# Transfers booked by their size in the ordering pass, and products of zeros by constants in TensorE's idle time of the first batch of heads

## The chip, the cores and the metric

One core of a Trainium2 chip runs the whole program in one launch. The metric is the device time in microseconds; the median of three runs of the kernel before is 1121.18 us (1121.18, 1116.87 and 2566.6). The core has five engines with queues of their own, each worked off strictly in order: TensorE (PE: products and transposes into PSUM), VectorE (DVE), ScalarE (ACT), GpSimd (POOL, used only for constants here) and SyncE (SP), which issues all transfers. An instruction that waits for a semaphore holds up everything behind it on its engine.

## The reference

Linear attention over a memory mixed with local causal attention, then two feed-forward layers on all 2304 rows:

```python
B, H, S, D = (4, 8, 576, 64)
scores = np.where(causal, -1e9, scale * q @ k.T)          # per batch and head
a = np.exp(scores - scores.max(-1)); a /= a.sum(-1) + 1e-09
local = a @ v
q_p = np.where(q > 0, q, np.exp(q) - 1.0) + 1.0
mem_out = (q_p @ M_prev) / ((q_p * z_prev).sum(-1) + 1e-06)
x = g * mem_out + (1 - g) * local                          # g = sigmoid(beta), per head
x = x.transpose(0, 2, 1, 3).reshape(B * S, H * D)           # 2304 x 512
h = x @ w_in;  x = (h * np.tanh(softplus(h))) @ w_out       # layer 1: 512 -> 2048 -> 512
h = x @ w_in2; out = (h * np.cos(h)) @ w_out2               # layer 2
```

## The kernel before

**Attention** works on 16 pairs of heads, four pairs for each batch (function `pair`, m = 0 to 15). For a pair, SyncE loads k, q, z, v and M (L328 to L347). PE transposes k and q (`ptk`, `ptq`, L368). In three groups (`slot`, s0, s1, s2) PE forms the scores (`s`, L461; the mask is added by products in bf16, L465; `sx`, L472), VectorE takes their maxima (`nm`, L486), ScalarE the exponentials (`p`, L502), VectorE scales them (L539). PE then transposes the probabilities in blocks of 128 (`t`, L554; 30 blocks in a pair), which ScalarE and VectorE copy to `PT`, and forms the products with the values (`pv`, L621). The result goes by `xs` to DRAM (`x1d`, L630).

**Feed-forward.** The weights of the layers come in an integer form (`raw`, L110 and L113), and VectorE and ScalarE decode each in five operations (`decode_w`, L125 to L142) into two parts; a product by x or by w takes three passes over such parts. The first layer has two halves. `block0` does the first half of its inner dimension for nine blocks of 256 rows: x is loaded from `x1d` (L666), split (ScalarE L285, VectorE L701), multiplied by w_in (`h`, L726), evacuated, put through Mish (ScalarE L738), split again (`G`, L746) and multiplied by w_out (`acc`, L769). A block can start when the pairs of its rows are done: block 0 after pairs 0 to 3. Blocks fill PE while later pairs run through their softmax. `late` does the second half of layer 1 (blocks 9 to 14 of 384 rows; L854, L934) and layer 2 (blocks 15 to 20; L854, L936).

**What sets the order.** Nothing of this is issued as the loops run. Each step is entered by `add` as a task with an engine (or two to choose from), a cost, its predecessors, a rank and the buffers that it takes. `arrange` (L175) then plays the program through: at each time it gives each free engine the ready task of lowest rank, books its cost, and the tasks' functions are called in the order that results. That fixes the order in each engine's queue. A transfer has a cost on SyncE and a `lag` after which its data count as landed, 2.0 to 4.0 us, whatever else is on the way. PE's clock is not part of the plan.

Of the kernel before, what the change touches and what calls it, by code (L numbers as in the profile page):

```python
# [10 lines left out]
F32 = mybir.dt.float32  # L11
F32R = mybir.dt.float32r
I32 = mybir.dt.int32
BF16 = mybir.dt.bfloat16
# [15 lines left out]
def tile_kernel(ctx: ExitStack, tc: tile.TileContext, q, k, v, M_prev, z_prev, beta,  # L30
                moe_w_in, moe_w_out, moe2_w_in, moe2_w_out, out):
    nc = tc.nc
# [3 lines left out]
    P = 128  # L36
# [5 lines left out]
    T0 = 256  # L42
# [54 lines left out]
    pools = {}  # L97
# [57 lines left out]
            made[cls] = self.n + 1  # L155

    class Task:
        __slots__ = ("eng", "cost", "fn", "deps", "rank", "takes", "func", "mode", "lag", "end", "n", "outs", "on")

    tasks = []  # L160
    slots_of = {}

    def add(eng, cost, fn, deps=(), rank=0.0, takes=(), uses=(), func=None, mode=0, lag=0.0):
        t = Task()
        t.eng, t.cost, t.fn, t.rank, t.takes = eng.split("/"), cost, fn, rank, list(takes)
        t.func, t.mode, t.lag, t.end, t.on = func, mode, lag, None, None
        t.deps = [d for d in deps if d is not None]
        for b in (*takes, *uses):
            b.users.append(t)
        tasks.append(t)  # L170
        return t

    SEM, SWITCH, TABLE, WAIT = 0.1, 0.12, 1.3, 2.5

    def arrange():  # L175
        outs = {}
# [20 lines left out]
        func, mode = "exp", 0  # L197
        now, order, left = 0.0, [], len(tasks)


# [13 lines left out]
        while left:  # L214
            nxt = None

            def later(x):
                nonlocal nxt
                if nxt is None or x < nxt:
                    nxt = x  # L220

            for e in ready:
                if free[e] > now:
                    later(free[e])
                    continue
                best = None
                for r in ready[e]:
                    rank, k, at, t = r
                    if t.on is not None:
                        continue  # L230
                    for b in t.takes:
                        f = at_free(b)
                        if f is None:
                            at = None
                            break
                        at = max(at, f)
                    if at is None:
# [12 lines left out]
                t = r[3]  # L250
                cost = t.cost[t.eng.index(e)] if isinstance(t.cost, tuple) else t.cost
                if e == "act" and t.func and t.func != func:
                    cost, func = cost + TABLE, t.func
                if e == "pe":
                    cost, mode = cost + (SWITCH if t.mode != mode else 0.0), t.mode
                t.on, t.end = e, now + cost
                free[e] = t.end
                for b in t.takes:
                    held[b.cls][turn[b.cls] % len(held[b.cls])] = b
                    turn[b.cls] += 1  # L260
                for x in t.eng:
                    ready[x] = [q_ for q_ in ready[x] if q_[3] is not t]
                order.append(t)
                left -= 1
                for d in outs.get(id(t), ()):
                    d.n -= 1
                    if not d.n:
                        put(d)
                later(t.end)
                if e == "host":  # L270
                    later(now)
            if left:
                assert nxt is not None, [(e, r[0], r[3].fn.__name__, [(b.cls, b.n, turn[b.cls]) for b in r[3].takes]) for e in ready for r in ready[e]][:40]
                now = max(now, nxt)
        return order

    def run(order):
        for t in order:
# [35 lines left out]
    x1_done = {}  # L314

    def pair(m):
# [29 lines left out]
            nc.sync.dma_start(out=mv[0:D], in_=M_prev[b, h0:h0 + 2].rearrange("h d e -> d h e"))  # L346
            nc.sync.dma_start(out=mv[D:P], in_=v[b, h0:h0 + 2, 0:D].rearrange("h p d -> p h d"))  # L347

        dk = add("sp", 0.9, f_k, rank=R, takes=[B_["k"]], lag=2.8)
        dq = add("sp", 1.3, f_q, rank=R, takes=[B_["q"]], lag=2.8)  # L350
        dz = add("sp", 0.5, f_z, rank=R + 5, takes=[B_["z"]], lag=2.5)
        dv = add("sp", 1.8, f_v, rank=R + 5, takes=[B_["v"], B_["mv"]], lag=2.5)


        got = {}
# [249 lines left out]
        def pv(x):  # L605
# [30 lines left out]
            x1_done[m, x] = add("sp", 0.4, f_out, [t_x], -1.0, [], [B_["xs"]], lag=2.0)  # L636
            return t_p, t_x

        p_0 = x_0 = None
# [48 lines left out]
    def block0(bi, prev):  # L688
        R = 10000.0 + 1000 * bi
        bx = Buf("x0")  # L690
        ld = add("sp", 0.5, lambda e: load_x(bi), x_ready(bi), -0.5, [bx], lag=3.0)
        sp = []
        for c in (0, 2):
            def f_hi(e, c=c):
# [98 lines left out]
        xa_done[bi] = add("sp", 0.5, lambda e: nc.sync.dma_start(out=xad[bi], in_=d["o"]), [e1], -0.5, [], [bo], lag=2.0)  # L793
        return lasts[1]


# [6 lines left out]
    def late(bi, s0):  # L803
# [24 lines left out]
        if p == 1:  # L828
            def f_xa(e):
                d["o"] = o = O(bi, NKC, T1)  # L830
                t = j * T1
                while t < (j + 1) * T1:
                    b, s_ = divmod(t, T0)
                    w = min(T0 - s_, (j + 1) * T1 - t)
                    nc.sync.dma_start(out=o[:, :, t - j * T1:t - j * T1 + w], in_=xad[b][:, :, s_:s_ + w])
                    t += w

            xa = add("sp", 1.0, f_xa, [t_host2] + [xa_done[b] for b in range(N0)], R0 - 30, [bo], lag=3.5)
        prev = [None] * na
        for k_, f in enumerate(fs):  # L840
            s = s0 + k_
# [100 lines left out]
        for c in range(na):  # L942
# [5 lines left out]
            else:  # L948
# [5 lines left out]
                def f_out(e, c=c):  # L954
# [5 lines left out]
                add("sp", 0.4, f_out, [outs[-1]], -0.5, [], [bo], lag=2.0)  # L960
        if p == 1:
            x2_done[j] = add("sp", 0.4, lambda e: nc.sync.dma_start(out=x2d[j], in_=d["o"]), outs, -0.5, [], [bo], lag=2.0)
# [37 lines left out]
    def f_g1(e):  # L1000
        nc.vector.tensor_scalar(out=ginv, in0=ginv, scalar1=1.0, scalar2=None, op0=ALU.add)

    t_b = add("sp", 0.4, f_beta, rank=0.5, lag=2.0)
    t_g0 = add("act", 0.4, f_g0, [t_b], 0.0, func="exp")
    t_ginv = add("dve", 0.2, f_g1, [t_g0], 0.0)

# [90 lines left out]
```

## Time and profile before

| | |
|---|---|
| runs | 1121.18, 1116.87, 2566.6 us; median 1121.18 |
| profiled execution | 1123.04 us, its span 1121.3 us |
| PE busy | 1068.7 us, 95% of the span |
| DVE, ACT busy | 750.6 us (67%), 578.0 us (52%) |
| DMA | 88.70 MB, mean 79 GB/s |
| chain of waits | PE 80%, DVE 11%, DMA 4%, ACT 3% |

Busy shares are means over the span. Stages are told apart by the pairs and blocks that run in them: pairs 0 to 3 up to 101.2 us, pair 4 and the first products of block 0 to 132.3, pairs 5 to 15 with blocks in between to 388.4, the last blocks of the first half to 515, and then `late`. The clock column of the profile gives PE's granted clock in tenths or hundredths of 2.4 GHz: 1.00 and 0.50 are its two levels, 2.4 and 1.2 GHz.

### The profile page before, as it was taken

To read this page: it belongs to the slowest core of one execution; us is meant where nothing else is said; L and a number is where in the kernel's file an instruction comes from. 1 tells how busy PE (TensorE), PEld (TensorE's weight loads), DVE (VectorE), ACT (ScalarE), POOL (GpSimd) and SP (SyncE) were. 2 spreads that over 40 slices of the span, in tenths; PEclk is the share of its full clock that TensorE was granted. 3 is DMA by queue.
4 is the path that set the end of the run, shared out by engine and by line. 5 is a ranking of instruction groups with operands and counts; after the bars stand their busy time and mean duration, and the time that the engine had idled before them with its cause. 6 is when DMAs were issued, how large, how long until landed. Compare 5 with 4: busy or idle time off the path is not lost.

```text
span 1121.3 us, 17518 instructions
## 1 busy us (share of the span) xinstructions
PE 1068.7 (95%) x6720; PEld 940.4 (84%) x6720; DVE 750.6 (67%) x1684; ACT 578.0 (52%) x1286; POOL 3.8 (0%) x19
## 2 busy tenths in 40 slices
PE   6888989999999989997999999999999999999998
PEld 4555767778787789997999999999999999999997
DVE  6787887787877568416841225898667666666664
ACT  4665666665666434333332333576556455554554
POOL 1000000000000000000000000000000000000000
PEclk9776989999999989999999999999999999999999
DMA  5454322323132156404741123600001010000000
GB/s 142 116 144 125 102 77 50 104 60 100 34 102 54 60 165 201 134 37 149 224 143 52 62 85 122 207 20 29 29 1 57 1 38 20 29 29 1 29 1 29
DMA packets 112852, 88.70 MB, mean 79 GB/s; under 512 B 65792, under 2 KB 103680, under 8 KB 112768
## 3 DMA queue, kind: packets, MB, share of 16 engines
q1 hardware_dynamic: 112768, 87.58, 26.0%
q8 instruction: 53, 0.87, 0.3%
q14 instruction: 31, 0.25, 0.1%
HBM read 68.69 MB, written 18.87 MB: 78 GB/s over the span
## 4 chain that ended last, share of the span: by engine, by line
PE 80%; DVE 11%; DMA 4%; ACT 3%; issue 1%; SPq 1%; ACTq 0%; DVEq 0%
PE h L854 26%; PE acc L936 18%; PE h L726 9%; PE acc L934 7%; PE acc L769 7%; PE t L554 4%; PE pv L621 3%; DVE nm L486 3%; PE s L461 3%; DMA x<-x1d 2%; DVE p L539 1%; PE ptq L368 1%; ACT p L502 1%; DVE PT L287 1%; DMA raw<-in_moe_w_out_dram 1%
## 5 line engine op out<-in xcount | busy, mean ns | idle before, releaser
L854 PE MATMUL h<-x,w 128*128 128x384 f32 x1728 | 345.7, 337 | 1.6 <-ACT g L870 1.6
L854 PEld LDWEIGHTS h<-x,w 128*128 128x128 f32 x1728 | 307.4, 188 | 17.6 <-ACT g L870 1.8
L936 PE MATMUL acc<-w,G 128*128 128x512 f32 x864 | 228.9, 393 | 0.0
L936 PEld LDWEIGHTS acc<-w,G 128*128 128x128 f32 x864 | 159.9, 188 | 21.8
L726 PE MATMUL h<-x,w 128*128 128x256 f32 x864 | 134.3, 296 | 8.3 <-ACT g L285 5.3
L921 DVE TENSOR_TENSOR G<-g,G 128x384 fp32r<-128x384 f32 x144 | 79.8, 555 | 90.8 <-ACT G L285 88.9
L769 PE MATMUL acc<-G,w 128*128 128x256 f32 x864 | 130.5, 291 | 1.7 <-DVE G L746 0.7
L726 PEld LDWEIGHTS h<-x,w 128*128 128x128 f32 x864 | 116.9, 199 | 13.2 <-ACT g L285 8.3
L934 PE MATMUL acc<-G,w 128*128 128x384 f32 x576 | 113.8, 337 | 3.9 <-DVE G L921 2.4
L769 PEld LDWEIGHTS acc<-G,w 128*128 128x128 f32 x864 | 113.1, 193 | 4.9 <-ACT o L285 1.8
L285 ACT ACTIVATE G<-g 128x384 fp32r<-128x384 f32 (+1 forms) x156 | 83.2, 534 | 65.0 <-DVE g L905 34.6
L502 ACT ACTIVATE p<-s,nm 128x64 f32<-128x64 f32 (+4 forms) x160 | 81.3, 516 | 47.7 <-DVE nm L486 20.1
L934 PEld LDWEIGHTS acc<-G,w 128*128 128x128 f32 x576 | 100.8, 188 | 5.4 <-DVE G L921 3.5
L554 PE MATMUL t<-ident,p 128*128 128x128 f32 (+1 forms) x480 | 86.3, 314 | 15.4 <-ACT PT L285 5.2
L554 PEld LDWEIGHTS t<-ident,p 128*128 128x128 f32 (+1 forms) x480 | 61.4, 160 | 29.4 <-ACT PT L285 11.8
L882 DVE TENSOR_SCALAR u<-hs 128x384 f32<-128x384 f32 x96 | 34.5, 359 | 71.3 <-ACT hs L285 68.6
L898 ACT ACTIVATE n<-n 128x384 f32<-128x384 f32 x96 | 50.2, 523 | 60.7 <-DVE n L894 60.7
L461 PE MATMUL s<-kT,qT 64*128 64x448 f32 (+4 forms) x320 | 68.7, 513 | 12.2 <-DVE nm L486 6.5
L486 DVE TENSOR_REDUCE nm<-s 128x2 f32<-128x1024 f32 (+4 forms) x80 | 62.5, 791 | 19.8 <-PE s L465 10.2
L905 DVE TENSOR_TENSOR g<-n,hs 128x384 f32<-128x384 f32 x96 | 53.3, 555 | 28.5 <-ACT n L901 28.4
L285 ACT ACTIVATE PT<-t 128x512 f32<-128x512 f32 (+3 forms) x100 | 46.9, 480 | 41.3 <-PE t L554 40.1
L870 ACT ACTIVATE g<-h 128x384 f32<-128x384 f32 x48 | 23.3, 488 | 84.7 <-PE h L854 83.9
(88 smaller groups left out, 1183.9 us busy)
## 6 DMA issues: line engine op xcount, KB each, us to landing
raw<-in_moe_w_in_dram SPq DMA_DIRECT2D x32, 512.0 KB, 4.4
raw<-in_moe_w_out_dram SPq DMA_DIRECT2D x32, 512.0 KB, 4.4
k<-in_k_dram SPq DMA_DIRECT2D x32, 144.0 KB, 2.8
x1d<-xs SPq DMA_DIRECT2D x32, 144.0 KB, 2.0
xad<-o SPq DMA_DIRECT2D x9, 512.0 KB, 2.8
x2d<-o SPq DMA_DIRECT2D x6, 768.0 KB, 3.2
x<-x2d SPq DMA_DIRECT2D x6, 768.0 KB, 4.3
out_dram<-o SPq DMA_DIRECT2D x18, 256.0 KB, 2.0
```

The costliest lines, as they stand in the source:

```text
L285: nc.scalar.activation(dst, src, AF.Copy, scale=1.0 if scale is None else scale)
L461: nc.tensor.matmul(o[:, j], qT[pr, s0:s0 + P], kT[pr, 0:main], start=True, stop=False)
L486: nc.vector.tensor_reduce(out=s["nm"][:, c], in_=s["sp"][i], axis=AX.X, op=ALU.max, negate=True)
L502: nc.scalar.activation(d["p", i][:, j, D + lo:D + hi], src, AF.Exp, bias=s["nm"][:, c, j:j + 1], scale=1.0, accum_out=s["sm"][:, 1 if part ...
L554: nc.tensor.transpose(ps[:, at:at + r], d["p", i][0:r, h, j * P:(j + 1) * P], ident[0:r, 0:r])
L726: nc.tensor.matmul(h[:, half // 2], w[:, a, 0, c * P:(c + 1) * P], x[:, e_, c, :], start=c == 0 and pi == 0, stop=c == NKC - 1 and pi == 2)
L769: nc.tensor.matmul(t[:, c], w[:, a, 1, n * P:(n + 1) * P], G[:, e_, half], start=f == 0 and pi == 0 and c == 0, stop=f == NFH - 1 and pi == 2,
L854: nc.tensor.matmul(q_["h"], w[:, a, 0, c * P:(c + 1) * P], x[:, e_, c, :], start=c == 0 and pi == 0, stop=c == NKC - 1 and pi == 2)
L905: nc.vector.tensor_tensor(out=q_["g"], in0=q_["n"], in1=q_["hs"], op=ALU.mult)
L921: ENG[e].tensor_tensor(out=q_["G"][:, 1], in0=q_["g"], in1=q_["G"][:, 0].bitcast(F32), op=ALU.subtract)
L934: nc.tensor.matmul(o, w[:, a, 1, c * P:(c + 1) * P], G[:, e_, :], start=st, stop=sp_)
L936: nc.tensor.matmul(o, G[:, a, c * P:(c + 1) * P], w[:, e_, 1, :], start=st, stop=sp_)
```

## The change

Two things are changed in the ordering pass. First, a transfer has a `size` in KB in place of a fixed lag: transfers are booked one after the other at 160 KB per us, and each counts as landed 2.0 us after its turn. Second, as long as no block of the feed-forward has begun, the pass looks at what it has given PE in the time just before; where this falls under a share, and no task is ready, it puts in a product of a constant by zeros, with 256 columns in bf16, into a PSUM buffer that nothing reads. The computation of the outputs is the same. All engines get another order, since the booked times differ.

```diff
+    RATE, LAND = 160.0, 2.0
...
                 if best is None:
+                    if e == "pe" and t_warm.on and not turn["h"]:
+                        while done and done[0][1] < now - 3.4:
+                            done.popleft()
+                        if sum(y - max(x, now - 3.4) for x, y in done) < 0.75 * 3.4:
+                            t = Task()
+                            t.eng, t.cost, t.fn, t.on, t.end = ["pe"], 0.12, f_dummy, "pe", now + 0.12
+                            free[e] = t.end
+                            done.append((now, t.end))
+                            order.append(t)
+                            later(t.end)
                     continue
...
+                if e == "pe":
+                    done.append((now, t.end))
+                if t.size:
+                    moved = max(moved, t.end) + t.size / RATE
+                    t.lag = moved - t.end + LAND
...
+    def f_warm(e):
+        warm["w"] = pools["h"].tile([P, 2, T0], F32, tag="h", name="warm")
+        warm["z"] = const.tile([P, T0], BF16, name="zeros")
+        nc.vector.memset(warm["z"], 0.0)
+
+    def f_dummy(e):
+        nc.tensor.matmul(warm["w"][:, 0], ident_b, warm["z"], start=True, stop=True)
+
+    t_warm = add("dve", 0.2, f_warm)
...
-        dk = add("sp", 0.9, f_k, rank=R, takes=[B_["k"]], lag=2.8)
-        dq = add("sp", 1.3, f_q, rank=R, takes=[B_["q"]], lag=2.8)
+        dk = add("sp", 0.9, f_k, rank=R, takes=[B_["k"]], size=288)
+        dq = add("sp", 1.3, f_q, rank=R, takes=[B_["q"]], size=352)
...
-        ld = add("sp", 0.5, lambda e: load_x(bi), [*need, t_host if bi == N0 else t_host2], R0 - 90, [bx], lag=3.5)
+        ld = add("sp", 0.5, lambda e: load_x(bi), [*need, t_host if bi == N0 else t_host2], R0 - 90, [bx], size=768)
...
-        ld = add("sp", 0.5, lambda e: fetch_next(), after, rank - 30.0, [bw], lag=4.0)
+        ld = add("sp", 0.5, lambda e: fetch_next(), after, rank - 30.0, [bw], size=512)
```

The other transfers are changed in the same way (z 64, v 320, `x1d` 144, x of block0 512, `xad` 512, `o` from `xad` 768, `x2d` 768, output rows 256 KB).

There are 187 products of zeros: 22 ahead of the transposes of the first keys, 12 ahead of those of the first queries, 120 in the rest of pairs 0 to 3, in runs of up to 19, and 33 in pair 4, up to the first product of block 0. Numbers in the names below are pair or block and part.

SyncE, the transfers after the first loads of pair 1, before (`raw0_1_1` is a part of the weights, `xs0` the result of pair 0):

```order
L328 DMA k2_337<-in_k_dram 96x6x64 x2
L338 DMA z2_381<-in_z_prev_dram 128x128
L332 DMA q2_421<-in_q_dram 128x2x64
L334 DMA q2_421<-in_q_dram 128x4x64 x2
L113 DMA raw0_1_1_437<-in_moe_w_out_dram 128x1024
L630 DMA x1d0_65<-xs0_446 128x288
```

and with the change:

```order
L358 DMA k2_400<-in_k_dram 96x6x64 x2
L113 DMA raw0_1_1_448<-in_moe_w_out_dram 128x1024
L362 DMA q2_511<-in_q_dram 128x2x64
L364 DMA q2_511<-in_q_dram 128x4x64 x2
L660 DMA x1d0_65<-xs0_508 128x288
L368 DMA z2_536<-in_z_prev_dram 128x128
```

The weights stand ahead of the queries of pair 2 now, and z of pair 2 behind the first result of pair 0.

PE, pair 4 from its last scores before (`h0_0` are block 0's first units, `t4` the transposes of pair 4's probabilities):

```order
L461 MATMUL s4_2_1197<-kT4_976,qT4_1098 128x192 x2
...
L726 MATMUL h0_0_0_1222<-x0_1169,w0_0_435 128x256 x12
L726 MATMUL h0_0_0_1222<-x0_1169,w0_1_642 128x256 x12
L554 MATMUL t4_3_1264<-ident_85,p4_0_1173 128x128 x4
L368 MATMUL ptk5_1_1272<-ident_85,k5_1013 128x96 x3
L726 MATMUL h0_0_1_1282<-x0_1169,w0_2_874 128x256 x6
L554 MATMUL t4_3_1294<-ident_85,p4_0_1173 128x128 x4
L726 MATMUL h0_0_1_1282<-x0_1169,w0_2_874 128x256 x6
L726 MATMUL h0_0_1_1282<-x0_1169,w0_3_925 128x256 x12
L554 MATMUL t4_0_1329<-ident_85,p4_0_1173 128x64 x2
L554 MATMUL t4_4_1332<-ident_85,p4_1_1176 128x128 x4
```

and with the change (`warm` are the products of zeros; of each run the first stands):

```order
L491 MATMUL s4_2_1374<-kT4_1112,qT4_1255 128x192 x2
...
L303 MATMUL warm_171<-zeros_172,ident_b_120 128x256
...
L584 MATMUL t4_3_1411<-ident_85,p4_0_1333 128x128 x4
...
L584 MATMUL t4_3_1440<-ident_85,p4_0_1333 128x128 x4
L584 MATMUL t4_0_1446<-ident_85,p4_0_1333 128x64 x2
...
L584 MATMUL t4_4_1478<-ident_85,p4_1_1336 128x128 x2
L756 MATMUL h0_0_0_1482<-x0_1325,w0_0_452 128x256 x6
```

Before, 24 products of block 0 stood ahead of the first transposes of `p4` and 84 ahead of the end of `pv4`; now none and 24. At the end of `pv15`, the last of the attention, 840 products of the first half stood ahead before, and now 834, of 1728.

ScalarE, after the last result of the attention, before (x9 is the x of the first late block, x6 that of block 6, `g0_5_0<-h0_5_0` the evacuation of PE's first unit of block 5):

```order
L285 ACTIVATE xs15_4596<-pv15_1_4603 128x288
L285 ACTIVATE g0_4_2_4614<-h0_4_3_4627 128x512
L738 ACTIVATE g0_4_2_4614<-g0_4_2_4614 128x1024
L285 ACTIVATE x9_4668<-x9_4668 128x768 x2
L285 ACTIVATE x6_4697<-x6_4697 128x512
L285 ACTIVATE g0_5_0_4745<-h0_5_0_4703 128x512
```

and with the change:

```order
L315 ACTIVATE xs15_4780<-pv15_1_4783 128x288
L315 ACTIVATE g0_4_2_4815<-h0_4_2_4744 128x512
L315 ACTIVATE g0_4_2_4815<-h0_4_3_4835 128x512
L768 ACTIVATE g0_4_2_4815<-g0_4_2_4815 128x1024
L315 ACTIVATE G0_4_2_4906<-g0_4_2_4815 128x512
L140 ACTIVATE w0_8_4916<-dec0_8_0_4888 128x512
L315 ACTIVATE g0_5_0_4934<-h0_5_0_4890 128x512
L140 ACTIVATE w0_8_4916<-dec0_8_1_4944 128x512
L315 ACTIVATE o4_4992<-acc0_4_0_4808 128x512
L140 ACTIVATE w0_9_4996<-dec0_9_0_4960 128x512
L768 ACTIVATE g0_5_0_4934<-g0_5_0_4934 128x1024
L315 ACTIVATE x9_4852<-x9_4852 128x768 x2
```

The evacuation of `h0_5_0` stood behind the casts of x9 and x6; now they stand behind it, with weight casts (`w0_8`, `w0_9`) between. In the same way the cast of x10 stood ahead of the activations g3 and g4 and stands behind them now, and the subtractions for x0 and x1 on VectorE moved from among the scaling of pair 4's first scores to behind it.

## Rows read from the trace of the kernel before

**Rows 1.** Stages: length; busy PE, PEld, DVE, ACT, POOL (count); clock; DMA share; GB/s.

```profile
0.00:31.60 31.60, 22.69 (x107) 13.95 (x107) 21.71 (x61) 15.71 (x45) 3.84 (x19) 1.00 0.51 128
31.60:50.20 18.60, 14.43 (x97) 9.32 (x95) 14.83 (x42) 11.60 (x36) 0.00 (x0) 0.76 0.46 124
50.20:77.20 27.00, 24.84 (x154) 15.40 (x153) 23.27 (x58) 16.64 (x49) 0.00 (x0) 0.73 0.43 116
77.20:101.20 24.00, 20.59 (x120) 12.80 (x116) 18.75 (x48) 13.64 (x40) 0.00 (x0) 0.64 0.43 118
101.20:132.30 31.10, 27.34 (x200) 22.17 (x198) 25.68 (x64) 18.42 (x45) 0.00 (x0) 0.84 0.47 129
132.30:388.40 256.10, 241.38 (x2003) 192.44 (x2000) 200.87 (x527) 161.46 (x439) 0.00 (x0) 0.99 0.28 73
388.40:411.00 22.60, 17.94 (x120) 17.54 (x121) 11.07 (x20) 7.55 (x12) 0.00 (x0) 0.85 0.59 187
...
501.00:565.00 64.00, 56.75 (x345) 54.46 (x344) 45.77 (x85) 26.11 (x46) 0.00 (x0) 1.00 0.58 184
565.00:1121.30 556.30, 552.75 (x2885) 514.74 (x2884) 339.38 (x700) 275.32 (x525) 0.00 (x0) 1.00 0.14 48
```

**Rows 2.** The same view, the stretches where matmuls run at the lower clock.

```profile
4.40:30.90 26.50, 21.99 (x97) 13.49 (x99) 20.42 (x55) 14.43 (x44) 0.22 (x2) 1.00 0.51 131
41.60:54.40 12.80, 11.20 (x49) 7.39 (x49) 11.17 (x30) 7.44 (x23) 0.00 (x0) 0.50 0.25 63
65.00:74.80 9.80, 9.42 (x41) 5.88 (x41) 8.32 (x22) 5.47 (x14) 0.00 (x0) 0.50 0.35 93
82.10:98.80 16.70, 14.84 (x68) 9.51 (x68) 14.27 (x41) 10.20 (x32) 0.00 (x0) 0.50 0.25 78
...
401.50:410.00 8.50, 6.47 (x31) 6.47 (x32) 6.53 (x11) 3.74 (x7) 0.00 (x0) 0.60 0.21 66
```

**Rows 3.** Timeline of PE: start, duration, instruction; in brackets the idle time before.

```profile
4.41 1.19 PE L368 MATMUL ptk<-ident,k 96*128 96x96 f32 x6 [4.41 <-DMA k<-in_k_dram]
...
7.74 1.86 PE L461 MATMUL s<-kT,qT 64*128 64x448 f32 x4 [0.47 <-ACT qT L285]
...
31.59 1.02 PE L461 MATMUL s<-kT,qT 64*128 64x448 f32 x4
...
65.21 2.92 PE L554 MATMUL t<-ident,p 64*128 64x64 f32 x12 [0.80 <-DVE PT L287]
...
71.94 1.23 PE L621 MATMUL pv<-PT,mv 128*64 128x288 f32 x4
...
403.53 1.65 PE L726 MATMUL h<-x,w 128*128 128x256 f32 x6 [3.97 <-ACT g L285]
...
530.78 2.18 PE L934 MATMUL acc<-G,w 128*128 128x384 f32 x11 [2.37 <-DVE G L921]
```

**Rows 4.** The chain of waits in order of time: start, duration, what.

```profile
32.31 5.27 DMA raw<-in_moe_w_out_dram
...
394.98 7.30 DMA x<-x1d
...
405.17 1.28 PE acc L769 x6
...
411.17 0.71 PE acc L769 x6
```

**Rows 5.** Timeline of DVE (columns as in rows 3).

```profile
1.33 0.55 DVE L77 CAST ident_b<-ident 128x128 bf16<-128x128 f32 x1 [0.47 <-POOL ident masks.py:199]
...
37.68 0.43 DVE L125 TENSOR_SCALAR dec<-raw 128x512 int32<-128x512 int32 x1 [0.88 <-DMA raw<-in_moe_w_out_dram]
...
110.69 1.29 DVE L701 TENSOR_TENSOR x<-x 128x512 fp32r<-128x512 f32 x2 [1.97 <-ACT x L285]
...
526.29 1.83 DVE L822 TENSOR_TENSOR x<-x 128x768 fp32r<-128x768 f32 x2 [5.51 <-ACT x L285]
```

**Rows 6.** Timeline of ACT (columns as in rows 3).

```profile
399.12 1.58 ACT L285 ACTIVATE x<-x 128x768 fp32r<-128x768 f32 x2 [3.09 <-DMA x<-x1d]
```

More of the change, by code (lines that the diff above doesn't have):

```diff
@@ L157, in tile_kernel, with add @@
     class Task:
-        __slots__ = ("eng", "cost", "fn", "deps", "rank", "takes", "func", "mode", "lag", "end", "n", "outs", "on")
+        __slots__ = ("eng", "cost", "fn", "deps", "rank", "takes", "func", "mode", "lag", "end", "n", "size", "on")
     tasks = []
     slots_of = {}
-    def add(eng, cost, fn, deps=(), rank=0.0, takes=(), uses=(), func=None, mode=0, lag=0.0):
+    def add(eng, cost, fn, deps=(), rank=0.0, takes=(), uses=(), func=None, mode=0, lag=0.0, size=0):
         t = Task()
         t.eng, t.cost, t.fn, t.rank, t.takes = eng.split("/"), cost, fn, rank, list(takes)
-        t.func, t.mode, t.lag, t.end, t.on = func, mode, lag, None, None
+        t.func, t.mode, t.lag, t.end, t.on, t.size = func, mode, lag, None, None, size
         t.deps = [d for d in deps if d is not None]
@@ L196, in arrange @@
         free = {e: 0.0 for e in ready}
-        func, mode = "exp", 0
+        func, mode, moved = "exp", 0, 0.0
+        done = deque()
         now, order, left = 0.0, [], len(tasks)
@@ L275, in arrange @@
         return order
+    warm = {}
+    def f_warm(e):
[5 more added lines that the diff above has]
+    t_warm = add("dve", 0.2, f_warm)
     def run(order):
@@ L347, in f_v @@
             nc.sync.dma_start(out=mv[D:P], in_=v[b, h0:h0 + 2, 0:D].rearrange("h p d -> p h d"))
-        dk = add("sp", 0.9, f_k, rank=R, takes=[B_["k"]], lag=2.8)
-        dq = add("sp", 1.3, f_q, rank=R, takes=[B_["q"]], lag=2.8)
-        dz = add("sp", 0.5, f_z, rank=R + 5, takes=[B_["z"]], lag=2.5)
-        dv = add("sp", 1.8, f_v, rank=R + 5, takes=[B_["v"], B_["mv"]], lag=2.5)
+        dk = add("sp", 0.9, f_k, rank=R, takes=[B_["k"]], size=288)
+        dq = add("sp", 1.3, f_q, rank=R, takes=[B_["q"]], size=352)
+        dz = add("sp", 0.5, f_z, rank=R + 5, takes=[B_["z"]], size=64)
+        dv = add("sp", 1.8, f_v, rank=R + 5, takes=[B_["v"], B_["mv"]], size=320)
         got = {}
@@ L635, in pv @@
             t_x = add("act/dve", c_both(w), f_xs, [t_p, x_0], R + 60, [B_["xs"]] if x == 0 else [], [bm] + ([B_["xs"]] if x else []))
-            x1_done[m, x] = add("sp", 0.4, f_out, [t_x], -1.0, [], [B_["xs"]], lag=2.0)
+            x1_done[m, x] = add("sp", 0.4, f_out, [t_x], -1.0, [], [B_["xs"]], size=144)
             return t_p, t_x
@@ L690, in block0 @@
         bx = Buf("x0")
-        ld = add("sp", 0.5, lambda e: load_x(bi), x_ready(bi), -0.5, [bx], lag=3.0)
+        ld = add("sp", 0.5, lambda e: load_x(bi), x_ready(bi), -0.5, [bx], size=512)
         sp = []
@@ L792, in block0 @@
         e1 = add("act/dve", c_both(512), lambda e: f_o(e, 1), [lasts[1], e0], RM + bi, [], [ba[1], bo])
-        xa_done[bi] = add("sp", 0.5, lambda e: nc.sync.dma_start(out=xad[bi], in_=d["o"]), [e1], -0.5, [], [bo], lag=2.0)
+        xa_done[bi] = add("sp", 0.5, lambda e: nc.sync.dma_start(out=xad[bi], in_=d["o"]), [e1], -0.5, [], [bo], size=512)
         return lasts[1]
@@ L836, in f_xa @@
                     t += w
-            xa = add("sp", 1.0, f_xa, [t_host2] + [xa_done[b] for b in range(N0)], R0 - 30, [bo], lag=3.5)
+            xa = add("sp", 1.0, f_xa, [t_host2] + [xa_done[b] for b in range(N0)], R0 - 30, [bo], size=768)
         prev = [None] * na
@@ L959, in late @@
                                 [ba[c]] + ([bo] if c else [])))
-                add("sp", 0.4, f_out, [outs[-1]], -0.5, [], [bo], lag=2.0)
+                add("sp", 0.4, f_out, [outs[-1]], -0.5, [], [bo], size=256)
         if p == 1:
-            x2_done[j] = add("sp", 0.4, lambda e: nc.sync.dma_start(out=x2d[j], in_=d["o"]), outs, -0.5, [], [bo], lag=2.0)
+            x2_done[j] = add("sp", 0.4, lambda e: nc.sync.dma_start(out=x2d[j], in_=d["o"]), outs, -0.5, [], [bo], size=768)
     slots_of.update({"q": 1, "k": 1, "v": 2, "z": 1, "mv": 2, "mn": 1, "ph": 2, "den": 3, "qT": 2, "kT": 2, "kd": 2, "PT": 1,
@@ L1001, in f_g1 @@
         nc.vector.tensor_scalar(out=ginv, in0=ginv, scalar1=1.0, scalar2=None, op0=ALU.add)
-    t_b = add("sp", 0.4, f_beta, rank=0.5, lag=2.0)
+    t_b = add("sp", 0.4, f_beta, rank=0.5, size=4)
     t_g0 = add("act", 0.4, f_g0, [t_b], 0.0, func="exp")
```

## The prediction

> **What bounds the kernel now.** I read the stages first [rows 1], because the share of busy time over the whole span (PE 95%) mixes stages with different limits. From 565 us to the end TensorE is busy 552.75 of 556.30 us: no order can shorten that half. The loss lies before 132 us, around the end of the attention (388 to 411: 17.94 of 22.60 busy) and where the first feed-forward pass ends (501 to 565: 56.75 of 64.00). In the 101.2 us of pairs 0 to 3 PE is busy 82.55 us, and a good part of that at half speed: in the stretches of [rows 2] it is busy 21.99, 11.20, 9.42 and 14.84 us while the clock is at 0.50, which is the 1.2 GHz level. In the first of them the clock column says 1.00, but the durations don't: four products of queries and keys took 1.86 us at 7.74 and 1.02 us at 31.59 [rows 3]. So some 57 us of PE's work ran at the lower level; at the higher it would be about 29 us shorter. VectorE is the next limit there: busy 21.71, 14.83, 23.27 and 18.75 us, so it leaves 22.6 us idle in 101.2 [rows 1]. No change of PE alone can take more than that from pairs 0 to 3.
>
> The second loss is that engines stand behind a transfer that the planner thought would be there sooner. The chain of waits has such pieces: a weight transfer from 32.31 to 37.6 and an x transfer from 394.98 to 402.3 [rows 4]. VectorE waits for the first until 37.68, 0.88 us with nothing to do, and a reduction of scores stands behind it in its queue. At 110.69 it waits 1.97 us for x [rows 5]. At 399.12 ScalarE waits 3.09 us for x9 [rows 6], with the evacuation that PE needs queued behind, so that PE waits 3.97 us and then works at the lower level until 410 [rows 2, 3]: six products took 1.28 us at 405.17 and 0.71 at 411.17 [rows 4].
>
> **The change, part by part.** It does two things in the ordering pass, and nothing to the computation: 187 products of zeros on PE, and another order on all engines. Prices against the profiled run, 1123.04 us for a span of 1121.3; that is 1.9 over the median of the runs, 1121.18.
>
> A product of zeros has 256 columns and a weight load of its own, like the products in [rows 4]: 0.71/6 = 0.12 us at the higher clock, 1.28/6 = 0.21 us at the lower.
>
> (a) The start. The identity is cast by 1.88 us [rows 5], so PE can begin zeros at about 2.1 us. 22 of them at 0.21 end at 6.8 us, where the keys were transposed from 4.41 us on [rows 3]; 12 more stand ahead of the queries: 1.4 to 2.6 us. The first scores come 3.8 to 5 us later. If the clock is up by then they win back 0.84 us on each of the two large groups (1.86 against 1.02) and a little on the small ones, 2 us in all. Between +3 and 0 (VectorE's first idle hides it); I take +1.5, near the middle, since the scores start the chain of the whole pair.
>
> (b) The weight transfer of pair 1 is now issued ahead of the next queries, not behind them. VectorE's wait goes. It is worth 0 to -3.8, all the idle time of VectorE in the stage 31.6 to 50.2 [rows 1]; I take the middle, -2, since the transfer's 5.27 us [rows 4] began only behind the queries. Queued behind it on SyncE are now the next queries, which pair 2 needs a pair later.
>
> (c) The clock in pairs 0 to 3. From above -22.6 (VectorE's idle), from below 0. The zeros stand mainly ahead of a pair's third group of scores and ahead of its first transposes; among the last twenty transposes of a pair, where the lower clock lasted, there are only 4 to 6 of them. So I expect the clock to hold through the scores and the first transposes and to fall later: half of the 29 us of PE's time. VectorE was busy 77 to 87% of the same stretches [rows 2], so less than half of it shortens the path: -6.
>
> (d) 120 zeros stand within pairs 0 to 3 beside those of the start: 14.4 us at the higher level, 25.6 at the lower. PE's idle time from 4.41 to 101.2 us is 14.2 us [rows 1]; that is their cover. They run as soon as PE reaches them, not when it would idle, so a run of ten can outlast its wait: +1.5, between 0 and +11.4 (25.6 - 14.2).
>
> (e) Pair 4 and the first block of the feed-forward. Before, 84 of its products lie ahead of the end of pair 4; now 24, and zeros stand where they were. The stage 101.2 to 132.3 then becomes like pair 3's, 24.0 us, less some 2.5 us from clock, plus 24 x 0.12 = 2.9 for the products: 24.4 against 31.1, -6.7. That also contains the wait for x at 110.69, whose subtraction is now behind the work on pair 4's scores. But the 60 products are owed: at the end of the attention 834 are done against 840, so pairs 5 to 15 take in 54 more, 6.5 us. That stage has 14.7 us of PE idle [rows 1], and some of them fall into it: +4.5 (0 to +6.5). Together -2.2, between +6.5 (pair 4 as long as before) and -6.7 (the idle time takes the 54).
>
> (f) The end of the attention. ScalarE now evacuates the first unit of block 5 before the casts of x9 and x6. PE's wait of 3.97 us goes, and with it the lower clock after it: 6.47 us of PE work from 401.5 to 410 [rows 2], half of it 3.2. What is late next is the decode of the first weights after the attention, which keeps VectorE at work until about the time the next unit needs it. -6 of 7.2; between -7.2 and 0.
>
> (g) The end of the first pass. ScalarE's cast of x10 moves behind two activations, so that VectorE's 5.51 us of idle before x10 [rows 5] no longer holds back the operand for which PE waited 2.37 us [rows 3]. Weight decodes take the cast's place on ScalarE, and they have transfers of their own: -2, between -3.8 and +2.
>
> (h) The rest of the order from 565 us on: nothing, PE being the bound with 3.6 us of idle in 556.
>
> Sum: +1.5 - 2 - 6 + 1.5 - 2.2 - 6 - 2 = -15.2 us. The profiled run would take 1107.8 us, the median about **1106 us**, 1.4% less. About 2% is what a measurement of this kernel can tell from no change: below 1098.8 or above 1143.6.
>
> **The clock and the transposes.** The planner counts every instruction of PE as activity, transposes too. Rows speak against it: from 65.0 to 74.8 us PE was busy 9.42 of 9.80 us at 0.50, with transposes from 65.21 on, and the clock stayed down until after the products of probabilities and values had begun at 71.94 [rows 2, 3]. With products alone, from 403.53 us on, it was up by 411.17 [rows 3, 4]. The Trainium skill says the same ("TensorE: Matmul & The Clock Gate", Part 4: PE-mode transpose): a transpose does not count as a busy PE in the way a product does. By that rule the zeros, sparse where the transposes are, could not hold the clock there; by the planner's own count they hold it throughout. By that rule the sum is rival 2's, by the planner's count rival 1's; my (c) stands between the two.
>
> **Rivals.**
> 1. The zeros hold the clock through pairs 0 to 3, and VectorE becomes the bound. For it: at the higher clock the zeros are 14.4 us, as much as PE's idle time. Against it: the stretch from 65.0 us. Then (c) is some 15 of the 22.6 us and (d) nothing: -25.7, about 1096 us. 0.15.
> 2. The clock falls in each pair as early as before, as transposes don't hold it. Then (c) is 0 or nearly, the rest as above: -9.2, about 1112 us. For it: the stretches of 65.0 and 82.1 us [rows 2]; against it: six to ten zeros now stand ahead of the third group of scores of three of these pairs, where none of them is near a transpose of probabilities. 0.17. It is what the Trainium skill's rule would make of it.
> 3. The transfers' new places only move the waiting: at 394 and 516 us the decode of the weights, for which VectorE is busy 45.77 of 64 us at 501 to 565, ends last instead of x. (f) and (g) are nothing: -7.2, about 1114 us. 0.12. That the order does not do what it says would look the same.
> 4. Slower than before: the clock stays at the lower level and the zeros are in the way. The 153 zeros after the first 34 are 32 us at 0.21, and their cover is 14.2 us of idle time in pairs 0 to 3 and 3.8 in pair 4 [rows 1]; they decide from where a run ends after the operand it fills for, some 2 us for ten. With +14.6 in (d), +3 in (a), 0 in (c), +4.5 in (e), -2 in (b) and -4 in (f) and (g): +16.1, about 1137 us. For it: many of the runs stand between transposes; against it: zeros are products, and a run of products did bring the clock up. 0.06.
>
> **Chances.** My forecast has 0.50. The range reaches from rival 1 to just above the old time, with the bounds of (d) and (e) against (c): 1092 to 1123 us. Faster by over 2%: most of rival 1 and a rest of the forecast's lower end, 0.15. Slower by over 2%: half of rival 4, 0.03. Within 2%: 0.82.
>
> **What would show it.** (a): keys transposed at 6 to 7 us, first exponential after 12.31. (b): no wait for raw weights before 40 us. (c): the clock at full level in the scores of pairs 1 to 4 and at 0.50 in the last transposes and first value products; the end of pair 3 at about 96 us instead of 101.2. (d): runs of zeros that end before their successor's operand. (e): the first feed-forward product only after 105 us, pair 4 done near 120. (f): no gap of PE over 1 us and no 0.50 between 380 and 410 us. (g): no wait of 2 us behind x10. It is wrong if the end of pair 3 does not move, or if PE's gap at the end of the attention only changes its releaser.

## The result, and the profile after

The changed kernel takes **1092.42 us** (median of four runs, 1091.78 to 1094.71); the kernel before took 1120.86 on the same chip. The ratio is **0.9762, 95% interval [0.9731, 0.9792]**: 2.4% faster, where 1.4% was forecast. Medians here and below take in a single far slower run where one fell (before 2566.6 us, first experiment 1175.19, third 1698.83), while the ratios leave it out. The profiled run takes 1091.78 us for a span of 1090.0, 31.3 us less than the span of before; some 2 us of that are the profiled run of before, which lay above its median.

Four lines of the page after: span, busy time, TensorE's clock in the 40 slices, the shares of the chain of waits.

```profile
span 1090.0 us, 17872 instructions
...
PE 1056.5 (97%) x6907; PEld 937.7 (86%) x6907; DVE 761.1 (70%) x1699; ACT 570.6 (52%) x1272; POOL 3.9 (0%) x19
...
PEclk9999999999999999999999999999999999999999
...
PE 85%; DVE 10%; ACT 3%; issue 1%; POOL 0%; ACTq 0%; POOLq 0%
```

A 9 in the clock's line means 0.9 or more; the one stretch at 0.50 behind the start lies at 44.7 to 48.1 us, in pair 1. No transfer is left in the chain (4% before). The stages after, in the columns of [rows 1]:

```profile
0.00:32.90 32.90, 26.47 (x204) 18.76 (x204) 23.48 (x64) 15.44 (x47) 3.87 (x19) 1.00 0.55 141
32.90:48.90 16.00, 13.42 (x105) 9.78 (x103) 14.84 (x41) 10.89 (x35) 0.00 (x0) 0.89 0.54 141
48.90:72.40 23.50, 20.98 (x175) 13.67 (x175) 22.67 (x59) 14.69 (x45) 0.00 (x0) 1.00 0.40 107
72.40:93.10 20.70, 17.24 (x145) 11.49 (x143) 19.38 (x49) 13.63 (x42) 0.00 (x0) 1.00 0.52 143
93.10:119.40 26.30, 23.28 (x201) 16.40 (x198) 25.55 (x64) 16.93 (x53) 0.00 (x0) 1.00 0.66 162
119.40:369.10 249.70, 241.77 (x2031) 195.37 (x2029) 199.98 (x525) 163.73 (x431) 0.00 (x0) 1.00 0.28 73
369.10:391.00 21.90, 21.21 (x169) 20.45 (x170) 12.52 (x22) 9.74 (x15) 0.00 (x0) 1.00 0.65 211
...
539.00:1090.00 551.00, 547.48 (x2856) 509.56 (x2854) 350.33 (x720) 271.68 (x516) 0.00 (x0) 1.00 0.15 50
```

Three stages of [rows 1] had a clock of 0.64 to 0.76; now one of the first four is at 0.89 and the others at 1.00. The waits of the engines for transfers up to 540 us come down to one line, a decode of VectorE at 374 us, around which PE is nowhere idle for more than 0.69 us (engine, line, what it waited for: us in total, times, longest):

```profile
DVE dec L125 <- DMA raw<-in_moe_w_in_dram: 5.7, 1, 5.7
```

Before, up to 565 us, ScalarE waited 22.4 us for x in ten places, and VectorE 9.4 for weights and 5.8 for queries.

The table gives each stage against the forecast, and the third experiment, which has exactly the order of after without the zeros. So "order" is its difference to before, "zeros" what is left. Pairs end here with their last product by the values, up to 0.2 us off the marks of [rows 1]:

| stage | before | after | change | order | zeros | forecast |
|---|---|---|---|---|---|---|
| pairs 0 to 3 | 101.2 | 93.2 | -8.0 | -2.2 | -5.8 | (a) to (d): -5 |
| pair 4 | 31.1 | 26.2 | -4.9 | -2.7 | -2.2 | (e): -6.7 |
| pairs 5 to 15 | 256.1 | 249.7 | -6.4 | -4.9 | -1.5 | (e): **+4.5** |
| to the store of the last block of the first half | 127.3 | 120.7 | -6.6 | -6.5 | -0.1 | (f): -6 |
| to the end | 605.6 | 600.2 | -5.4 | -5.4 | 0 | (g): -2 |
| span | 1121.3 | 1090.0 | -31.3 | -21.7 | -9.6 | -15.2 |

Each column is one execution, and the first row of "order" is not firm: the tenth experiment has the order of before up to there, and its pair 3 ended at 95.2 us, not at 101.2 (see the last section).

### The profile page after: what moved, and what is told of

Same layout as the page of the kernel before. It is cut to its first block, busy times and chain, and to the rows that moved or that the text cites. A ratio compares the mean times of both kernels' runs of the same rounds, so it can differ in the third digit from the quotient of the medians.

```text
span 1090.0 us, 17872 instructions
## 1 busy us (share of the span) xinstructions
PE 1056.5 (97%) x6907; PEld 937.7 (86%) x6907; DVE 761.1 (70%) x1699; ACT 570.6 (52%) x1272; POOL 3.9 (0%) x19
## 2 busy tenths in 40 slices
DMA packets 112852, 88.71 MB, mean 81 GB/s; under 512 B 65792, under 2 KB 103680, under 8 KB 112768
## 3 DMA queue, kind: packets, MB, share of 16 engines
q1 hardware_dynamic: 112768, 87.58, 26.9%
## 4 chain that ended last, share of the span: by engine, by line
PE 85%; DVE 10%; ACT 3%; issue 1%; POOL 0%; ACTq 0%; POOLq 0%
PE h L884 28%; PE acc L966 18%; PE acc L964 9%; PE h L756 9%; PE acc L799 8%; PE pv L651 4%; PE t L584 4%; DVE nm L516 3%; PE s L491 3%; DVE p L569 2%; ACT p L532 1%; PE ptq L398 1%; DVE PT L317 1%; PE warm L303 1%; DVE p L545 1%
## 5 line engine op out<-in xcount | busy, mean ns | idle before, releaser
L884 PEld LDWEIGHTS h<-x,w 128*128 128x128 f32 x1728 | 307.3, 188 | 17.2 <-ACT g L900 1.8
L756 PE MATMUL h<-x,w 128*128 128x256 f32 x864 | 128.9, 288 | 2.7 <-ACT g L315 1.6
L756 PEld LDWEIGHTS h<-x,w 128*128 128x128 f32 x864 | 111.6, 190 | 6.9 <-ACT g L315 4.5
L532 ACT ACTIVATE p<-s,nm 128x448 f32<-128x448 f32 (+4 forms) x160 | 81.4, 517 | 43.7 <-DVE nm L516 16.4
L584 PE MATMUL t<-ident,p 128*128 128x128 f32 (+1 forms) x480 | 74.1, 280 | 10.5 <-DVE PT L317 6.3
L516 DVE TENSOR_REDUCE nm<-s 128x2 f32<-128x128 f32 (+4 forms) x80 | 62.4, 793 | 21.8 <-PE s L495 11.2
L935 DVE TENSOR_TENSOR g<-n,hs 128x384 f32<-128x384 f32 x96 | 53.2, 555 | 26.3 <-ACT n L931 26.2
L584 PEld LDWEIGHTS t<-ident,p 128*128 128x128 f32 (+1 forms) x480 | 53.3, 142 | 21.2 <-DVE PT L317 8.8
L491 PE MATMUL s<-kT,qT 64*128 64x512 f32 (+4 forms) x320 | 61.8, 472 | 9.6 <-DVE nm L516 5.9
L315 ACT ACTIVATE hs<-h 128x384 f32<-128x384 f32 x96 | 47.1, 490 | 39.2 <-PE h L884 36.5
```

The lines of the kernel that those rows point to most:

```text
L315: nc.scalar.activation(dst, src, AF.Copy, scale=1.0 if scale is None else scale)
L491: nc.tensor.matmul(o[:, j], qT[pr, s0:s0 + P], kT[pr, 0:main], start=True, stop=False)
L516: nc.vector.tensor_reduce(out=s["nm"][:, c], in_=s["sp"][i], axis=AX.X, op=ALU.max, negate=True)
L532: nc.scalar.activation(d["p", i][:, j, D + lo:D + hi], src, AF.Exp, bias=s["nm"][:, c, j:j + 1], scale=1.0, accum_out=s["sm"][:, 1 if part ...
L584: nc.tensor.transpose(ps[:, at:at + r], d["p", i][0:r, h, j * P:(j + 1) * P], ident[0:r, 0:r])
L756: nc.tensor.matmul(h[:, half // 2], w[:, a, 0, c * P:(c + 1) * P], x[:, e_, c, :], start=c == 0 and pi == 0, stop=c == NKC - 1 and pi == 2)
```

## The experiments

All run beside the kernel before; ratios are to it, with 95% intervals. Spans and stages are of each one's profiled run. Line numbers are those of the kernel after, or shifted by one to four (those of the kernel before in the tenth).

**1 to 3: the two parts, and the zeros in a fixed order.**

```diff
 e1_sizes_only, against after
-                    if e == "pe" and t_warm.on and not turn["h"]:
+                    if False:
 e2_zeros_only, against after (each of 13 transfers)
-        dk = add("sp", 0.9, f_k, rank=R, takes=[B_["k"]], size=288)
+        dk = add("sp", 0.9, f_k, rank=R, takes=[B_["k"]], lag=2.8)
 e3_order_no_zeros, against after
     def f_dummy(e):
+        return
```

> The transfers are booked by size as in the changed kernel, and no zeros are inserted (the planner chooses its own order without them: 12 feed-forward products ahead of the end of pair 4). Theory A (the zeros' clock gives what pairs 0 to 4 won, the booking what came after): pair 3 ends at 99 to 102 us, the stage of pair 4 is 26 to 28 us long, pairs 5 to 15 about 250 us, the first half of the program ends 11 to 15 us after the changed kernel's; 1103 to 1107 us. Theory B (the booking gives nearly all, the clock was never on the path because VectorE is): pair 3 ends at 94 to 96 us; 1092 to 1096 us. Theory C (the zeros give nearly all, the booking only moves waits): 1115 to 1121 us.

> The zeros are inserted as in the changed kernel, the transfers have the fixed delays of the kernel before again. Theory A: pair 3 ends at 93 to 95 us with the clock at its higher level in nearly all of it, VectorE again waits for the weight transfer near 32 us, pairs 5 to 15 take 253 to 256 us as before, and the gap at the end of the attention is back; 1105 to 1110 us. Theory B: pair 3 ends at 99 to 101 us although the clock is up; 1117 to 1121 us. Theory C: 1092 to 1097 us.

> Exactly the changed kernel's order on every engine, but the 187 products of zeros are not issued. That takes the clock away and nothing else. Theory A: in pairs 0 to 3 the clock is at 0.50 in the transposes again, pair 3 ends at 99 to 101 us instead of 93.1, pair 4's stage is 1 to 3 us longer than 26.3, and from 119 us on nothing differs; 1100 to 1104 us. Theory B: pair 3 ends at 93 to 95 us; 1091 to 1094 us. That the zeros were in the way on balance would show as a time under 1090.

Measured: booking alone 1109.36 us, 0.9912 [0.9875, 0.9949]; zeros alone 1112.76, 0.9939 [0.9908, 0.9969]; the order of after without its zeros 1101.61, 0.9836 [0.9776, 0.9897]. Theory A holds for the third (pair 3 ends at 99.0) and fails for the first two: each part alone gives 0.6 to 0.9%, both 2.4%. In a fixed order the zeros are worth 8 to 9 us (9.2 by the medians, 1101.61 - 1092.42, which come from two series of runs; 8.3 by the two ratios); the rest is order. The first and the third both run without zeros, and differ by 8 us by order alone: pairs 0 to 3 end at 103.6 us instead of 99.0, and without zeros in the plan 918 feed-forward products fall into pairs 5 to 15 instead of 810, and the stage takes 273.1 us instead of 251.2. At 0.15 us a product (129 us for 864) the 108 more are 16 us, so some 6 us are lost there, with a fall of the clock near 215 us; the other stages make up for part of it. Why that order fits worse stays open.

What the zeros do in the fixed order is seen in pair 0. Windows (columns of [rows 1]) of the third experiment, then of the kernel after:

```profile
24.00:27.00 3.00, 2.74 (x12) 1.73 (x10) 2.83 (x8) 1.43 (x4) 0.00 (x0) 0.50 0.57 175
27.00:30.00 3.00, 3.00 (x12) 1.52 (x13) 2.23 (x5) 1.55 (x4) 0.00 (x0) 0.50 0.04 8
```

```profile
24.00:27.00 3.00, 2.65 (x18) 1.75 (x18) 2.98 (x9) 1.77 (x4) 0.00 (x0) 1.00 0.32 96
27.00:30.00 3.00, 2.84 (x25) 1.92 (x24) 3.00 (x7) 1.98 (x5) 0.00 (x0) 1.00 0.21 82
```

PE's timeline after, there:

```profile
22.60 1.36 PE L303 MATMUL warm<-zeros,ident_b 128*128 128x256 bf16 x11
23.89 1.36 PE L584 MATMUL t<-ident,p 64*128 64x64 f32 x10
25.50 1.50 PE L584 MATMUL t<-ident,p 128*128 128x128 f32 x8 [0.25 <-ACT PT L315]
27.17 0.44 PE L584 MATMUL t<-ident,p 128*128 128x128 f32 x2 [0.16 <-ACT PT L315]
27.44 0.38 PE L303 MATMUL warm<-zeros,ident_b 128*128 128x256 bf16 x2
27.66 0.38 PE L584 MATMUL t<-ident,p 128*128 128x128 f32 x2
```

Eleven zeros (0.12 us each) stand ahead of the pair's last 22 transposes and only two within them, and the clock holds through all of them. Without the zeros PE is as busy at 0.50, and gets 12 instructions done in each 3 us instead of 18 and 25.

**4 and 5: the price of zeros.**

```diff
 e4_no_zeros_at_start: f_dummy returns for its first 34 calls
 e8_zeros_doubled: f_dummy issues its product twice
```

> The changed kernel's order, without the first 34 products of zeros (22 ahead of the keys' transposes, 12 ahead of the queries'). If the start's zeros cost what my term (a) said, the keys are transposed at about 4.4 us again instead of 6.69, the first scores come 1 to 2.5 us sooner though at the lower clock (1.86 us instead of 1.02 for four), and pair 0 ends 1 to 2 us sooner: 1090 to 1091.5 us. If they pay for themselves by the clock, pair 0 ends at the same time or later: 1092 to 1094 us.

> The changed kernel's order with every product of zeros issued twice: 187 more, 22 us of TensorE's time at 0.12 us each. If zeros lie in time that TensorE has to spare beside VectorE (my term d near its lower bound), pair 3 ends at 93 to 96 us and the time is 1092 to 1096 us. If they are in the way (the mechanism of my rival 4), about half or more of the 22 us appears: pair 3 ends after 100 us and the time is 1102 to 1114 us.

Measured: 1091.54 us, 0.975 [0.9711, 0.9789], and 1099.78, 0.9851 [0.9814, 0.9887]. Without the first 34 the first exponential starts at 12.01 us, with them at 13.12, yet pair 0 ends at 33.4 and 33.0: the start's zeros win back by the clock what they cost, and no more. Doubled zeros cost 7.9 us of the span, and neither range of their expectation holds: pair 3 ends at 99.7. Of the 7.9 us 5.3 are there by the end of pair 0 (2.8 by its first scores, which start at 12.93 instead of 10.18). From there to the end of pair 4 the doubled kernel, then the one after:

```profile
38.30:127.30 89.00, 84.34 (x727) 61.05 (x727) 82.75 (x210) 55.95 (x174) 0.00 (x0) 1.00 0.50 135
```

```profile
33.00:119.40 86.40, 74.83 (x617) 51.23 (x617) 82.34 (x210) 56.13 (x174) 0.00 (x0) 0.98 0.53 139
```

110 more products make PE busy 9.5 us longer and the stretch only 2.6: behind pair 0 the zeros lie for the most part in time that PE has to spare.

**6 to 9: which transfers, and whether size matters.**

```diff
 e5_x_booked_only (e6_x_not_booked: with "not"); the fixed lags stand beside the sizes
                     moved = max(moved, t.end) + t.size / RATE
+                    if t.takes and t.takes[0].cls in ("x0", "x", "o2"):
                         t.lag = moved - t.end + LAND
 e9_longer_delays: no sizes; lag=2.8, 2.5, 3.0, 3.5, 4.0 become 5.3, 5.0, 5.5, 6.0, 6.5
 e11_rate_180: RATE, LAND = 180.0, 2.0
```

> Zeros as in the changed kernel; every transfer still occupies the planner's queue by its size, but only the loads of x (and of the stored first half that is added to it) are believed to land when that queue says; queries, keys, values and weights have the fixed delays of before. Theory X (the gain of the booking is that ScalarE no longer stands in front of an x that has not landed): no wait of ScalarE for x of over 1 us from 100 to 560 us, though VectorE still waits for queries a few times; 1093 to 1099 us, near the changed kernel. Theory Q (the queries and weights carry it): 1105 to 1111 us, near the zeros alone (1112.8).

> The complement: zeros, queries, keys, values and weights believed by size, the loads of x by the fixed 3.0 and 3.5 us of before. Theory X: ScalarE waits for x again for 10 to 25 us in all, among them 3 to 7 us at the end of the attention and as much at the end of the first feed-forward pass; 1104 to 1111 us. Theory Q: 1093 to 1099 us.

> Zeros as in the changed kernel, but fixed delays again, each load's 2.5 us longer than before (5.0 to 6.5 us instead of 2.5 to 4.0), without a queue. Theory P (the planner only had to be more cautious; size and queue don't matter): the waits of ScalarE for x and of VectorE for queries and weights fall from over 20 us to a few, and the time is 1092 to 1098 us. Theory S (lateness comes from queueing behind other transfers, which no constant follows): waits for x, queries or weights of 2 to 6 us remain at the places where several transfers stand in a row, and the time is 1101 to 1112 us.

> The changed kernel with the planner's transfer rate at 180 instead of 160 KB per us; sizes, queue and zeros stay. It gives another order of the same kind. If the gain comes from the booking as such, it stays within 3 us of the changed kernel: 1090 to 1096 us, without waits for x over 1 us. If a good part of it is the luck of one order, the time is 1098 to 1108 us.

Measured: only x booked 1111.87 us, 0.9946 [0.9925, 0.9967]; all but x 1118.63, 1.0011 [0.9989, 1.0032]; longer fixed delays 1106.74, 0.9883 [0.9844, 0.9923]; the other rate 1094.1, 0.9776 [0.9738, 0.9814]. Neither X nor Q holds: half a booking is worth no more than the zeros alone (0.9939), or less. With only x booked pair 3 ends at 98.3 us instead of 93.2, and the stage to the last store takes 132.5 instead of 120.7; with all but x pair 3 ends at 92.2, but pairs 5 to 15 take 268.0 instead of 249.7. The largest waits for transfers up to 560 us in the first, the second, the third and the fourth of them:

```profile
DVE dec L125 <- DMA raw<-in_moe_w_in_dram: 11.2, 3, 10.1
DVE dec L125 <- DMA raw<-in_moe_w_out_dram: 8.3, 3, 5.6
DVE mn L428 <- DMA q<-in_q_dram: 7.8, 3, 3.6
```

```profile
ACT x L316 <- DMA x<-x1d: 23.0, 9, 4.2
```

```profile
ACT x L315 <- DMA x<-x1d: 11.8, 6, 4.1
```

```profile
DVE dec L125 <- DMA raw<-in_moe_w_in_dram: 3.3, 1, 3.3
```

The transfers share one queue (q1 moves 87.58 of the 88.71 MB), and whichever kind the plan believes too early is waited for. Two and a half microseconds more for each halve the waits for x against the 22.4 us of before (theory S: three of 2.8 to 4.1 us stay, behind several loads in a row). Another rate gives another order, and 1.7 us more: a second booked order keeps the gain. That any would is not shown; the first and the third experiment, booked alike, lie 8 us apart.

**10: the casts of x alone.** The order of before; only ScalarE's casts of x stand two instructions later.

```diff
 e7_casts_later, against before
-    run(arrange())
+    run(later_casts(arrange()))   # f_hi behind the next two other tasks of ScalarE, dependents behind it
```

> The kernel before, with fixed delays and no zeros: TensorE's and SyncE's orders are untouched; only the casts of x on ScalarE stand behind the next two other instructions of ScalarE, and the subtractions that need them as much later on VectorE. It takes the evacuations and activations out from behind the transfers of x and changes nothing else. Theory X: the waits behind x9 and x6 at 399 and behind x10 at 525 us no longer hold up TensorE: -6 for the first (my term f), -2 (my term g) to -5 for the second, nothing before 130 us but the 1.97 us wait; 1106 to 1113 us against about 1120. Theory M (the wait only moves, since the decode of weights ends last): 1117 to 1121 us.

Measured: 1119.22 us, 1.001 [0.9989, 1.0031]. That is theory M by the time, though not by the reason that it gave. In its profile ScalarE's waits for x are down from 22.4 to 6.6 us, and its stage from the end of attention to the store of the last block is 125.7 us, 1.6 less than before; from there to the end it is 2.6 less, and pairs 5 to 15 take 2.9 more. PE's timeline shows why it isn't 6:

```profile
400.77 0.44 PE L854 MATMUL h<-x,w 128*128 128x384 f32 x1 [0.31 <-ACT x L285]
404.00 1.97 PE L854 MATMUL h<-x,w 128*128 128x384 f32 x5 [2.80 <-DVE x L822]
```

With the evacuation freed, PE reaches the products of x9 itself, which stand early in its own queue, and waits there for 2.80 us in place of the 3.97 of [rows 3]. The order after has it late on both engines. SyncE's issue of the three x loads, ScalarE's evacuation and casts, and PE's first product of x9 after:

```profile
371.80 5.42 SPq L696 DMA_DIRECT2D x<-x1d  x3
```

```profile
379.83 0.60 ACT L315 ACTIVATE g<-h 128x512 f32<-128x512 f32 x1 [0.94 <-PE h L756]
...
387.56 2.60 ACT L315 ACTIVATE x<-x 128x768 fp32r<-128x768 f32 x4
```

```profile
392.41 1.24 PE L884 MATMUL h<-x,w 128*128 128x384 f32 x6
```

The transfers start no earlier than before (2.6 us after the last evacuation of `pv` began before, 2.7 after). The instructions that need them come later: the casts 15.8 us after the issue (8.1 before), the product 20.6.

**11: is VectorE the bound in pairs 0 to 3?**

```diff
 e10_less_decode, against after: in decode_w, op 1 and op 2
+            if moe == 0 and 2 * f + part < 9:
+                return
```

> The changed kernel's order; of the decode of the first nine weight parts the two instructions that join the low and high bits are left out (18 x 0.68 = 12.2 us of VectorE's 80.4 in the first 93 us; those weights are then wrong). Nothing else is changed, though the raw buffer is free some us sooner. Theory V (with the clock held VectorE is the bound in pairs 0 to 3): pair 3 ends 5 to 10 us sooner, at 83 to 88 us, and the time is 1082 to 1088 us. Theory E (TensorE's own chain of transposes, scores and the exponentials is the bound): pair 3 ends less than 2.5 us sooner; 1090 to 1092 us.

Measured: 1090.15 us, 0.9734 [0.9688, 0.978]. Theory E: pair 3 ends at 93.1 us (93.2 with the whole decode). The same marks as in the stages after (pair 2 with the end of 1, and pair 3):

```profile
48.90:72.40 23.50, 20.94 (x174) 13.37 (x173) 18.14 (x48) 15.05 (x46) 0.00 (x0) 1.00 0.41 111
72.40:93.10 20.70, 17.17 (x135) 12.21 (x131) 16.48 (x44) 12.57 (x40) 0.00 (x0) 0.92 0.46 131
```

VectorE's share there falls from 95% to 78% (42.05 to 34.62 us of 44.2) and little gets shorter: pair 2 ends at 70.8 us instead of 72.4, and pair 3, with its clock at 0.92, loses that again. Two of the four runs, at a mean clock of 1.000 against 0.998, took 1088.7 and 1088.9 us, so without such a fall some 3 us may be VectorE's, not the 5 to 10 of theory V. Much of its high share was decodes that could wait. That the bound is the chain of scores, exponentials and transposes through three engines is what is left over; no run tests it.

No version with the right outputs clearly beat the one after: the fourth ties with it (0.975), and the eleventh leaves out part of the decode.

## Why the prediction was right, and by half too small

The direction was right, and the range just held: 1092.42 us stand at its lower end, and "faster by over 2%" had a chance of 0.15. The size was twice the forecast, and that the range held so large a miss is luck. Of the 16 us of the span that the sum is short, 11 are the pairs 5 to 15 of (e), 3 are pairs 0 to 3 and 3 are (g); pair 4 gave 2 less than forecast.

(a) **Mis-sized:** +1.5 against nothing that can be told. The first exponential came 0.8 us later, at 13.12, but the pair's end 2 us sooner, at 33.0; without the start's zeros it is 33.4. The two large groups of scores ran in 1.02 and 1.08 us.

(b) -2: the wait is gone, the price is open. No raw weight is waited for before 40 us. The stage up to the first scores of pair 2 is 16.0 us instead of 18.6, but it holds less: 20 products of pair 0 (`pv`, 2.3 us) stood behind the first scores of pair 1 and stand ahead of them now. From the start, pair 2's first scores come at 48.9 us instead of 50.2, and at 50.0 in the third experiment. With zeros in the plan, pair 3 ends at 92.2 to 93.2 us where weights and queries are booked (seventh, ninth, after) and at 96.3 to 99.1 where they are not (second, sixth, eighth), 3 us or more between them, though in orders that differ in more than this.

(c) **Failed in part.** I expected the clock to fall in the late transposes, from 9.42 us of transposes at 0.50 [rows 2, 3]. It fell there in pair 1 alone, for 3.4 us, and held in the others. That row showed a clock that had fallen before it, not that transposes let it fall. With (d) small (doubling the zeros cost 2.6 us behind pair 0), the zeros gave -5.8 in pairs 0 to 3, where (a), (c) and (d) together said -3. That is rival 1 in the clock, but not in its other half: VectorE did not become the bound.

(e) **Failed: the sign.** Pair 4 took 26.2 us where I had 24.4. I charged the owed products 4.5 us in pairs 5 to 15, and not even the step's lower bound of 0 was low enough: the idle time took them, and the stage fell by 6.4 us. Most of it sat in one place, pair 5. Before, that pair had few products to stand between its transposes, because pair 4 had used them up (24 against 72 now); its stretch before and after:

```profile
132.30:158.00 25.70, 20.55 (x151) 14.95 (x150) 23.27 (x59) 15.22 (x45) 0.00 (x0) 0.87 0.39 103
```

```profile
119.40:145.00 25.60, 24.22 (x204) 19.55 (x203) 23.99 (x56) 16.91 (x43) 0.00 (x0) 1.00 0.43 110
```

The same time holds 53 more instructions of PE, at full clock. From the end of pair 4 to that of pair 6 it is 47.5 us instead of 52.7, with 150 feed-forward products instead of 126: 5.2 of the 6.4 us. I had taken the 14.7 us of idle time as spread over the 256. The 5.4 us for which VectorE waited for queries in this stage went too, of which I spoke nowhere; what it is worth by itself is not shown.

(f) -6: right, -6.6. PE's largest gap there is 0.69 us, the clock 1.00. But the mechanism is wider than I put it: moving the casts alone gains nothing that can be told over the whole kernel; PE's own product of x9 had to move as well.

(g) **Mis-sized:** -2 against -5.4. PE's one wait left after the store is this:

```profile
490.72 2.35 PE L884 MATMUL h<-x,w 128*128 128x384 f32 x12 [1.60 <-ACT g L900]
```

The 2.37 us of [rows 3] are gone in full and two waits of 0.67 behind casts with them (PE idle 8.4 us of 605.6 before, 4.4 of 600.2). That is 4.0 of the 5.4 us; the other 1.4 are busy time of PE, 597.2 against 595.8, and stay open. I had kept back half for decodes that would be late next; none was.

(h) right. Rival 2 is refuted by the clock, rival 3 by the missing waits, rival 4 by the time and the clock.

## What to carry to other kernels

An order planned ahead is as good as its landing times: book transfers that share a queue by their size, all of them or none, since the one kind still believed too early takes the waits over. Where a stall stands in several in-order queues, moving the instruction of one engine can just move the stall to the next. Work held back from one stage need cost nothing if a later one has a hole for it, so look for that hole in the trace, pair by pair, before charging it. A length between two marks compares two orders only if the same work lies between the marks.

## What the runs showed of the hardware

**The clock through transposes.** In the third experiment, without zeros, PE did nothing but transposes from 63.5 to 72.4 us, and they held the clock:

```profile
63.50:72.40 8.90, 5.56 (x40) 3.77 (x36) 8.62 (x26) 6.32 (x21) 0.00 (x0) 1.00 0.39 92
```

The Trainium skill ("TensorE: Matmul & The Clock Gate", Part 4: PE-mode transpose) says that a transpose does not count as a busy PE in the way a product does; this stretch speaks against it. In bringing a fallen clock up, transposes did it in one case and not in another. In the third experiment PE had nothing but transposes from 84.1 to 94.9 us; the clock stood at 0.50 from 82.9 us and at 1.00 from 93.1, which the durations show too (ten took 2.49 us, the last two 0.44):

```profile
89.27 2.49 PE L585 MATMUL t<-ident,p 128*128 128x128 f32 x10
91.93 1.92 PE L585 MATMUL t<-ident,p 128*128 128x128 f32 x8 [0.17 <-ACT PT L316]
94.01 0.44 PE L585 MATMUL t<-ident,p 128*128 128x128 f32 x2 [0.17 <-DVE PT L318]
```

In the kernel before the clock stayed down through 6.7 us of them (65.2 to 71.9 us [rows 3]), with PE busy 5.62 of the first 5.80, and came up only at 75.2, behind the products that followed:

```profile
65.20:71.00 5.80, 5.62 (x22) 3.87 (x22) 5.70 (x16) 3.52 (x10) 0.00 (x0) 0.50 0.28 63
```

So what the prediction read from that stretch is no rule. What decides between the two is not shown.

**The same work, two clocks.** The tenth experiment leaves the order of before untouched up to the end of pair 3. In its pair 2 the clock stayed at 1.00:

```profile
63.90 1.52 PE L554 MATMUL t<-ident,p 64*128 64x64 f32 x10 [0.80 <-DVE PT L287]
```

After the same 0.80 us of idle time, the same transposes took 2.92 us for twelve in [rows 3]: in one run the clock fell, in the other it did not, and pair 3 ended at 95.2 instead of 101.3 us. So one order can lose the clock in one execution and keep it in another. Runs of the kernel before spread from 1110.04 to 1121.71 us (25 runs on one chip); the kernel after took 1091.78 to 1094.71, the one with doubled zeros 1099.68 to 1100.2. That the clock and the late transfers make this spread was not tested.
